# A sliding-window attention and mixture-of-depths kernel: the first batch by head groups, and the next batch's preparation spread over its blocks

## The chip, the cores and the metric

The kernel runs on one core of a Trainium2 chip. A core has five instruction streams: TensorE (PE in the profile, its weight loads PEld), VectorE (DVE), ScalarE (ACT), GpSimd (POOL) and SyncE (SP), which here only issues loads. The metric is the time of one execution on the device in microseconds (us); lower is better. The time of the kernel before is the median of three runs.

## The reference

Four batches, eight heads, 768 positions, head size 64. Attention sees a window of 128 positions and the first 4 positions ("sinks"). Then, per batch, the 128 rows with the highest gate score go through a two-layer MLP and are added back.

```python
scores = scale * np.matmul(q, k.transpose(0, 1, 3, 2))
keep = is_sink | in_window            # pos < 4, or 0 <= row - col < 128
scores = np.where(keep, scores, -1000000000.0)
a = softmax(scores)
x = np.matmul(a, v)                   # laid out (B, S, H * D) = (4, 768, 512)
...
scores = np.einsum('bsd,d->bs', x, w_gate)
out = x.copy()
for b in range(B):
    top_idx = np.argpartition(-scores[b], capacity)[:capacity]   # 128 rows
    xe = x[b, top_idx]
    ye = np.maximum(xe @ w1, 0.0) @ w2        # w1 512x1024, w2 1024x512
    g = 1.0 / (1.0 + np.exp(-scores[b, top_idx]))
    out[b, top_idx] = xe + g[:, None] * ye
```

## The kernel before

**Tiling.** A batch is worked in six blocks `j` of 128 positions, a step `(b, j)` of the main loop (lines 540 to 577) each, 24 in all. The eight heads are four pairs `hp`, and two groups `g` of four heads (pairs 0 and 1, pairs 2 and 3).

**Before a batch can start**, q and k of a head pair are loaded (`kf`, `qf`), cast to bf16 (`kb`, `qb`, lines 125 to 131: in batch 0 by ScalarE and VectorE, later by GpSimd, which uses an `affine_select` that selects everything as a copy), transposed by TensorE into PSUM (`trp`, line 252) and copied out as `KT` (VectorE, line 257) and `QT` (ScalarE, line 259). The first four columns of K^T go into `ksk` by two small VectorE copies for each pair (line 261).

**A step.** `scores` (lines 270 to 299) makes the score tile of the next block for both groups: products `sc` (line 282), masks added by a product with the identity (line 293), exp on ScalarE into `pt` (line 299). Then come the value products of this block: `pv_sinks` (line 316) with `psk`, the exp of the sink scores (`sink_scores`, lines 301 to 307, once per batch in block 0), and `vsk`, the sinks' values (`pack_sinks`, line 148); and `pv` (line 326), 64 products of 128 by 65 for both groups. VectorE divides by the sum (`rz` line 332, `x` line 335), GpSimd issues the write of `x` to the output (line 340), VectorE reduces `x` with the gate vector to a column of gate scores `scol` (line 347, `junk` is its unused product).

**Selection.** `compare` (lines 352 to 361) spreads a block's scores along the columns (`bc` on TensorE, `sbc` on ScalarE) and counts on VectorE who is larger (`cm`, `row`). `moe_steps` of the batch before runs in three steps: `cs` and the permutation `E` (line 377), then `se`, `idx` and the gather `xe`, then `xeT`. `mlp_steps` has two: `hps` (line 419), and `ye` (line 425) with the scattered addition. The steps are placed by hand: selection in blocks 1, 2 and 4; the MLPs at (2,4), (3,0), (3,1), (3,2), (3,4) and (3,5). The last batch's selection and MLP are `moe_last` (lines 435 to 509), the tail. `keep_warm` (line 77) issues matmuls whose result is not used.

**Order.** Each engine and SP's queue carry out their instructions in the order in which the program writes them. Start-up (lines 524 to 529) casts and transposes all four pairs and makes the scores of block 0. Pairs 0 and 1 of the next batch are cast and transposed in block 3, pairs 2 and 3 in block 4: the casts are written before the values of that block, the transposes after them (lines 552 to 564).

**Loads.** `load` lets only a few transfers be under way: a load waits until the third one before it (the fourth in batch 0) has landed. Batch 0 has q and k in pieces of two heads, all in front of v, which comes in six pieces of 128 positions with all heads; the two small loads of the sinks' values stand after v's second piece. Batches 2 and 3 load q and k in pieces of four heads. The buffers are 3 for q and k (four heads each) and 3 for weights; batch 3 has its weight loads around its q and k loads.

Of the kernel before, what the change touches and what calls it, by code (L numbers as in the profile page):

```python
# [9 lines left out]
FP32 = mybir.dt.float32  # L10
# [21 lines left out]
def kernel(  # L32
# [17 lines left out]
    ws = ctx.enter_context(tc.tile_pool(name="ws", bufs=3))  # L50
    qkp = ctx.enter_context(tc.tile_pool(name="qkp", bufs=3))
# [3 lines left out]
    pp = ctx.enter_context(tc.tile_pool(name="pp", bufs=3))  # L55
    xp = ctx.enter_context(tc.tile_pool(name="xp", bufs=4))
# [35 lines left out]
    def load_qk(b, parts):  # L92
        st = BatchState()
        st.b = b
        st.kq = {}
        st.qf, st.kf = [], []
        if b == 3:
            load_w(0)
            load_w(1)
        n = 4 // parts  # L100
        for g in range(2):
            for lst, nm in ((st.kf, "kf"), (st.qf, "qf")):
                lst.append(qkp.tile([128, 4, NB, D], FP32, name=nm, tag=nm))
            for i in range(parts):
                for src, lst in ((k, st.kf), (q, st.qf)):
                    h0 = 4 * g + n * i
                    load(
                        flight=4 if b == 0 else 3,
                        out=lst[g][:, n * i:n * i + n, :, :].rearrange("p h c d -> p h (c d)"),
                        in_=src[b, h0:h0 + n, :, :].rearrange("h (p c) d -> p h (c d)", c=NB))  # L110
        if b == 3:
            load_w(2)
            load_w(3)
        return st

    def casts(st, hp):
        kb = qbp.tile([128, NB, 2, D], BF16, name="kb", tag="kb")
        qb = qbp.tile([128, NB, 2, D], BF16, name="qb", tag="qb")
        h0 = 2 * (hp % 2)
        ks = st.kf[hp // 2][:, h0:h0 + 2, :, :]  # L120
        qs = st.qf[hp // 2][:, h0:h0 + 2, :, :]
        ko = kb[:, :, :, :].rearrange("p c h d -> p h c d")
        qo = qb[:, :, :, :].rearrange("p c h d -> p h c d")
        if st.b == 0:
            nc.scalar.copy(out=ko, in_=ks)  # L125
            nc.vector.tensor_copy(out=qo, in_=qs)
        else:
            for o, i in ((ko, ks), (qo, qs)):
                for e in range(2):
                    nc.gpsimd.affine_select(out=o[:, e, :, :], in_=i[:, e, :, :], compare_op=ALU.is_ge, fill=0.0,  # L130
                                            base=0, pattern=[[0, NB], [0, D]], channel_multiplier=0)
        st.kq[hp] = (kb, qb)

    def load_v(st):
        b = st.b
        st.v = vbuf[b % 2]
        st.vsk = vsk[b % 2]
        for c in range(NB):
            load(out=st.v[:, c, :, 0:D], in_=v[b, :, c * 128:(c + 1) * 128, :].rearrange("h p d -> p h d"),
                 flight=4 if b == 0 else 3)  # L140
            if c == 1:

                raw = vsr[b % 2]
                for R in range(2):
                    nc.sync.dma_start(out=raw[64 * R:64 * R + 4 * NSINK, :], in_=v[b, 4 * R:4 * R + 4, 0:NSINK, :])
# [6 lines left out]
    st0 = load_qk(0, 2)  # L152
# [21 lines left out]
    load_v(st0)  # L174


    trif = cp.tile([128, 3, 64], FP32, name="trif", tag="trif")
# [15 lines left out]
    iota_i = cp.tile([128, 128], I32, name="iota_i", tag="iota_i")  # L193
# [50 lines left out]
    def transposes(st, hp):  # L244
        if not hasattr(st, "QT"):
            st.QT = tp.tile([128, HP, S], BF16, name="QT", tag="QT")
            st.KT = tp.tile([128, HP, S], BF16, name="KT", tag="KT")
            st.ksk = ksk[st.b % 2]
# [11 lines left out]
        for e in range(2):  # L260
            nc.vector.tensor_copy(  # L261
                out=st.ksk[64 * e:64 * e + 64, hp, 8 * (hp % 2) + 4 * e:8 * (hp % 2) + 4 * e + 4],
                in_=st.KT[64 * e:64 * e + 64, hp, 0:NSINK])
# [6 lines left out]
    def scores(st, kc, g):  # L270
        nq = 256 if kc + 1 < NB else 128
        if g == 0:
            st.pt[kc] = pp.tile([128, H, 256], FP32, name="pt", tag="pt")
        pt = st.pt[kc]
# [22 lines left out]
        po = pt[:, 4 * g:4 * g + 4, :].rearrange("p (a e) n -> p e a n", e=2)  # L297
# [3 lines left out]
    def sink_scores(st):  # L301
        st.psk = sp.tile([128, 512], FP32, name="psk", tag="psk")
        sk = ps.tile([128, 512], FP32, name="sk", tag="ps")
        for hp in (0, 2, 1, 3):
            nc.tensor.matmul(out=sk[es[hp // 2], :], lhsT=st.ksk[:, hp, :], rhs=st.QT[:, hp, 256:S],
                             start=(hp % 2 == 0), stop=(hp % 2 == 1), skip_group_check=True)
        nc.scalar.activation(out=st.psk[:, :], in_=sk[:, :], func=ACT.Exp, scale=0.125)

    def pv_sinks(st, j):
        st.xg = [x_ps.tile([128, 4, VS], FP32, name="xg", tag="xg") for _ in range(2)]  # L310
        if j < 2:
            return
        for m in range(2):
            for g in range(2):
                q0 = (j - 2) * 128 + 64 * m
                nc.tensor.matmul(out=st.xg[g][es[m], :, :], lhsT=st.psk[es[g], q0:q0 + 64],  # L316
                                 rhs=st.vsk[es[g], :, :], start=True, stop=False, skip_group_check=True)

    def pv(st, j, g):
        xg = st.xg[g]  # L320
        terms = [(j, 0)] if j == 0 else [(j - 1, 128), (j, 0)]
        for hh in range(4):
            h = 4 * g + hh
            for kc, off in terms:
                for m in range(2):
                    nc.tensor.matmul(out=xg[es[m], hh, :],  # L326
                                     lhsT=st.pt[kc][:, h, off + 64 * m:off + 64 * m + 64],
# [5 lines left out]
        if g == 0:  # L333
            st.x = xp.tile([128, DM], FP32, name="x", tag="x")
        nc.vector.tensor_tensor(  # L335
            out=st.x[:, 256 * g:256 * g + 256].rearrange("p (h d) -> p h d", h=4),
            in0=xg[:, :, 0:D], in1=rz[:, :, :].to_broadcast((128, 4, D)), op=ALU.mult)

    def finish_block(st, j):
        nc.gpsimd.dma_start(out=out[st.b, j * 128:(j + 1) * 128, :], in_=st.x[:, :])  # L340
        if st.b == B - 1:
            if j == 0:
                st.xb = ws.tile([128, NB, DM], BF16, name="xb", tag="wf")
            nc.gpsimd.affine_select(out=st.xb[:, j, :], in_=st.x[:, :], compare_op=ALU.is_ge, fill=0.0,
                                    base=0, pattern=[[0, DM]], channel_multiplier=0)
        junk = sp.tile([128, DM], FP32, name="junk", tag="junk")
        nc.vector.tensor_tensor_reduce(  # L347
            out=junk[:, :], in0=st.x[:, :], in1=wgb[:, :], scale=1.0, scalar=0.0,
# [86 lines left out]
    def moe_last(st):  # L435
# [68 lines left out]
        yo = sp.tile([128, DM], FP32, name="yo", tag="junk")  # L504
# [7 lines left out]
    def start_state(st):  # L512
        st.pt = {}
        st.cm = {}
# [5 lines left out]
    units = [(b, j) for b in range(B) for j in range(NB)]  # L520
    with tc.manual_schedule(engines={ENG.PE, ENG.DVE, ENG.Activation, ENG.Pool, ENG.SP}):
        start_state(st0)
        keep_warm(10)
        for g in range(2):
            for hp in (2 * g, 2 * g + 1):
                casts(st0, hp)
                transposes(st0, hp)
                keep_warm(4)
            scores(st0, 0, g)
        gen = None  # L530

        def step():
            if gen is not None:
                next(gen, None)

        prep = {3: (0, 1), 4: (2, 3)}
        w_casts = {(2, 2): (0, 1), (2, 3): (2, 3), (2, 5): (4, 5), (3, 0): (6, 7)}
        mlp = {(2, 4): (0,), (3, 0): (0,), (3, 1): (1,), (3, 2): (1,), (3, 4): (2,), (3, 5): (2,)}
        mlps = {}
        for u, (b, j) in enumerate(units):  # L540
            st = states[b]
            if j == 0 and b + 1 < B:
                states[b + 1] = load_qk(b + 1, 2 if b == 0 else 1)
                load_v(states[b + 1])
            nxt = units[u + 1] if u + 1 < len(units) else None
            if nxt:
                if nxt[1] == 0:
                    start_state(states[nxt[0]])
                for g in range(2):
                    scores(states[nxt[0]], nxt[1], g)  # L550
            pv_sinks(st, j)
            hps = prep.get(j, ()) if b + 1 < B else ()
            for hp in hps:
                casts(states[b + 1], hp)
            for g in range(2):
                pv(st, j, g)
            if j == 1:
                pack_sinks(st)
            if j == 0:
                sink_scores(st)  # L560
            if j in (2, 4):
                step()
            for hp in hps:
                transposes(states[b + 1], hp)
            for i in w_casts.get((b, j), ()):
                cast_w(i)
            if u:
                pb, pj = units[u - 1]
                compare(states[pb], pj)
            if j == 1:  # L570
                step()
            for i in mlp.get((b, j), ()):
                next(mlps[i], None)
            finish_block(st, j)
            if j == 0 and b > 0:
                gen = moe_steps(states[b - 1])
                mlps[b - 1] = mlp_steps(states[b - 1])
        moe_last(states[B - 1])
# [35 lines left out]
```

## Time and profile before

| | us |
|---|---|
| median of 3 runs | 156.34 (154.6 to 157.71) |
| the profiled execution's own time | 159.9 |
| its span, first to last instruction | 158.2 |
| TensorE busy in it | 133.1 |
| VectorE busy | 108.0 |
| ScalarE busy | 82.5 |
| GpSimd busy | 60.5 |

The page gives busy time for each engine, the span in 40 slices (3.96 us each) with the busy share in tenths, the granted TensorE clock and the transfers, the chain of work that ended last, and groups of instructions by line with their mean time and with what ended the idle time in front of them. The trace behind it gives the same for any stretch, and a timeline. Of VectorE's 108.0 us, line 261 has 12.9 in 32 copies of 64x4 elements. The queue of loads moved 23.37 MB in 35440 packets, and 26096 of all 38413 packets are under 512 B. "Issue" as a releaser means that the profile shows nothing that the engine waited for.

### The profile page before, as it was taken

What the parts mean: (1) busy time and instruction counts of PE and PEld (TensorE: products, weight loads), DVE (VectorE), ACT (ScalarE), POOL (GpSimd) and SP (SyncE); (2) the same over time, 40 slices, a digit from 0 to 9 for tenths busy, and PEclk for the clock granted to TensorE, in tenths of its full rate; (3) what the DMA queues carried; (4) which work ended last, traced back from release to release, by engine and by line L of the source; (5) the groups of instructions that cost most, each with busy time, mean ns of one, the idle gap of its engine ahead of it and who ended that gap; (6) DMA issues with size and microseconds to landing.
All of it is one profiled execution on the core that took longest, in us unless ns stands there. A gap on an engine that the chain in (4) does not pass through costs nothing.

```text
span 158.2 us, 6573 instructions
## 1 busy us (share of the span) xinstructions
PE 133.1 (84%) x2857; PEld 100.8 (64%) x2857; DVE 108.0 (68%) x305; ACT 82.5 (52%) x168; POOL 60.5 (38%) x111
## 2 busy tenths in 40 slices
PE   6967999879599859883999975899899999999940
PEld 2533687768386657572878864698578777865810
DVE  3774356579987835999587879787959728667110
ACT  3456596553658505725375572769975464320310
POOL 7100011797111109941011199970446229207220
PEclk9997899999999987999599999599999999999998
DMA  4999989999899989999982139991108026405221
GB/s 162 322 331 200 220 271 343 286 297 229 167 385 389 311 187 213 394 386 374 339 312 77 70 51 321 278 216 45 68 2 193 15 37 109 161 4 67 70 66 66
DMA packets 38413, 31.78 MB, mean 201 GB/s; under 512 B 26096, under 2 KB 34672, under 8 KB 38384
## 3 DMA queue, kind: packets, MB, share of 16 engines
q1 hardware_dynamic: 35440, 23.37, 52.0%
q0 software_dynamic: 2944, 8.00, 17.1%
q8 instruction: 22, 0.36, 1.0%
q14 instruction: 7, 0.06, 0.1%
HBM read 24.41 MB, written 7.34 MB: 201 GB/s over the span
## 4 chain that ended last, share of the span: by engine, by line
PE 58%; DVE 14%; issue 12%; ACT 5%; POOL 4%; DMA 2%; POOLq 1%; ACTq 0%
PE xg L326 22%; PE w L77 8%; PE sc L282 5%; PE xg L316 5%; DVE KT L257 5%; DVE ksk L261 5%; PE trp L252 4%; PE hps L419 4%; PE ye L425 3%; PE sc L293 3%; ACT pt L299 2%; DVE x L335 2%; DMA xr<-out_dram,idx 2%; PE bc L354 2%; POOL qb L130 1%
## 5 line engine op out<-in xcount | busy, mean ns | idle before, releaser
L326 PEld LDWEIGHTS xg<-vbuf,pt 128*64 128x64 f32 x1408 | 45.3, 142 | 12.9 <-issue 11.7
L326 PE MATMUL xg<-vbuf,pt 128*64 128x65 f32 x1408 | 49.2, 228 | 3.8 <-issue 3.8
L299 ACT ACTIVATE pt<-sc 128x512 f32<-128x512 f32 (+1 forms) x96 | 46.6, 579 | 7.9 <-PE sc L293 7.8
L340 POOL DMA_DIRECT2D out_dram<-x x24 | 16.3, 679 | 59.0 <-DVE x L335 55.5
L332 DVE RECIPROCAL rz<-xg 128x4 f32<-128x4 f32 x48 | 8.6, 180 | 23.6 <-PE xg L326 23.1
L282 PE MATMUL sc<-QT,KT 64*64 64x192 bf16 (+3 forms) x384 | 19.2, 253 | 6.1 <-DVE KT L257 4.1
L358 DVE SCALAR_TENSOR_TENSOR cm<-sbc,scol,tie 128x128 bf16<-128x128 f32 (+5 forms) x24 | 19.3, 804 | 4.5 <-ACT sbc L355 4.5
L259 ACT COPY QT<-trp 128x768 bf16<-128x768 bf16 x16 | 12.4, 800 | 18.7 <-PE trp L252 18.7
L335 DVE TENSOR_TENSOR x<-xg,rz 128x256 f32<-128x256 f32 x48 | 20.4, 425 | 1.8
L347 DVE CUSTOM_DVE_ANT_0 junk<-x,wgb 128x512 f32<-128x512 f32 x24 | 20.2, 843 | 0.6 <-DMA wgb<-in_moe_w_gate_dram 0.6
L257 DVE COPY KT<-trp 128x768 bf16<-128x768 bf16 x16 | 15.3, 954 | 3.5 <-PE trp L252 3.2
L282 PEld LDWEIGHTS <-KT 64*64 64x64 bf16 x384 | 9.4, 108 | 12.2 <-issue 8.1
L293 PE MATMUL sc<-msk,ident_b 64*64 64x256 bf16 (+1 forms) x352 | 16.9, 252 | 0.0
L77 PE MATMUL w<-warm 128*128 128x512 bf16 x49 | 15.1, 454 | 1.3 <-DVE warm L72 1.3
L355 ACT COPY sbc<-bc 128x128 f32<-128x128 f32 x24 | 6.6, 275 | 14.1 <-PE bc L354 12.6
L261 DVE COPY ksk<-KT 64x4 bf16<-64x4 bf16 x32 | 12.9, 404 | 0.8
L130 POOL TENSOR_SCALAR_AFFINE_SELECT kb<-kf 128x384 bf16<-128x384 f32 x24 | 13.2, 576 | 0.1
L252 PE MATMUL trp<-ident_b,kb 128*128 128x128 bf16 x96 | 8.7, 231 | 5.1 <-ACT kb L125 2.7
L130 POOL TENSOR_SCALAR_AFFINE_SELECT qb<-qf 128x384 bf16<-128x384 f32 x24 | 12.9, 558 | 0.0
L316 PE MATMUL xg<-vsk,psk 64*64 64x260 f32 x128 | 12.1, 431 | 0.0
L252 PEld LDWEIGHTS <-kb 128*128 128x128 bf16 x96 | 6.3, 103 | 7.8 <-ACT kb L125 4.2
L293 PEld LDWEIGHTS <-ident_b 64*64 64x64 bf16 x352 | 10.3, 112 | 0.0
(99 smaller groups left out, 146.6 us busy)
## 6 DMA issues: line engine op xcount, KB each, us to landing
vbuf<-in_v_dram SPq DMA_DIRECT2D x24, 256.0 KB, 5.8
out_dram<-x POOLq DMA_DIRECT2D x24, 256.0 KB, 4.6
wf<-in_moe_w_dram SPq DMA_DIRECT2D x4, 1024.0 KB, 8.3
kf<-in_k_dram SPq DMA_DIRECT2D x8, 384.0 KB, 4.4
qf<-in_q_dram SPq DMA_DIRECT2D x8, 384.0 KB, 5.2
kf<-in_k_dram SPq DMA_DIRECT2D x4, 768.0 KB
qf<-in_q_dram SPq DMA_DIRECT2D x4, 768.0 KB
wgb<-in_moe_w_gate_dram SPq DMA_DIRECT2D x1, 256.0 KB
```

The source lines that it names most:

```text
L77: nc.tensor.matmul(out=w[:, :], lhsT=warm[:, 0:128], rhs=warm[:, :], start=True, stop=True)
L130: nc.gpsimd.affine_select(out=o[:, e, :, :], in_=i[:, e, :, :], compare_op=ALU.is_ge, fill=0.0, base=0, pattern=[[0, NB], [0, D]], channel ...
L252: nc.tensor.transpose(out=trp[:, c, :], in_=src[:, c, :, :].rearrange("p h d -> p (h d)"), identity=ident_b[:])
L257: nc.vector.tensor_copy(out=o, in_=i)
L261: nc.vector.tensor_copy(out=st.ksk[64 * e:64 * e + 64, hp, 8 * (hp % 2) + 4 * e:8 * (hp % 2) + 4 * e + 4], in_=st.KT[64 * e:64 * e + 64, h ...
L282: nc.tensor.matmul(out=sc[e][es[kh], hh, q0:q1], lhsT=st.KT[es[e], hp, k0:k0 + 64], rhs=st.QT[es[e], hp, kc * 128 + q0:kc * 128 + q1], sta ...
L293: nc.tensor.matmul(out=sc[e][es[kh], :, 64 * s0:64 * s1].rearrange("p h (s n) -> p h s n", n=64), lhsT=ident_b[es[e], es[e]], rhs=m[es[e], ...
L299: nc.scalar.activation(out=po[:, e, :, 0:nq], in_=sc[e][:, :, 0:nq], func=ACT.Exp, scale=0.125)
L316: nc.tensor.matmul(out=st.xg[g][es[m], :, :], lhsT=st.psk[es[g], q0:q0 + 64], rhs=st.vsk[es[g], :, :], start=True, stop=False, skip_group_ ...
L326: nc.tensor.matmul(out=xg[es[m], hh, :], lhsT=st.pt[kc][:, h, off + 64 * m:off + 64 * m + 64], rhs=st.v[:, kc, h, :], start=(j < 2 and hh ...
L335: nc.vector.tensor_tensor(out=st.x[:, 256 * g:256 * g + 256].rearrange("p (h d) -> p h d", h=4), in0=xg[:, :, 0:D], in1=rz[:, :, :].to_bro ...
L347: nc.vector.tensor_tensor_reduce(out=junk[:, :], in0=st.x[:, :], in1=wgb[:, :], scale=1.0, scalar=0.0, op0=ALU.mult, op1=ALU.add, accum_ou ...
```

## The change

Batch 0 runs twice through its six blocks, first for heads 0 to 3 and then for heads 4 to 7. A new function `unit(b, j, gs)` is a step for the groups `gs`; for batch 0 it is called with one group, for the others with both. Start-up casts and transposes pairs 0 and 1 alone; pairs 2 and 3 of batch 0 are cast in blocks 3 and 4 of the first pass and transposed in front of the values of its block 5. The loads follow: q and k of pairs 0 and 1, the sinks' values, v of heads 0 to 3 in half pieces, q and k of pairs 2 and 3, v of heads 4 to 7. The loads of batch 1 are written between the two passes.

In the later batches the casts of a next pair stand at blocks 2, 3, 4 and 5, one pair each. Pair 0 is transposed in block 3 and pair 1 in block 4, in front of that block's values; pairs 2 and 3 in block 5, behind them. The next batch's block 0 has its scores in two parts: group 0 in front of the values of block 5, group 1 at the very end of that step. The `ksk` copies go from VectorE to GpSimd. All q and k loads are of two heads, with 4 buffers; the weights have 4 buffers and their loads stand behind batch 3's q and k, ahead of its v. Selection steps are in blocks 1, 2 and 3, that of block 2 in front of its values. The MLP halves are at (3,0), (3,1), (3,2) twice, (3,3) and (3,4), and the weight casts at (2,5) and (3,0), four each. `pt` is a tile for one group (6 buffers), `x` has 8 buffers, `xg` and its sink products are made for one group at a time, `junk` is bf16, and `trif`, `iota_i` and `yo` use the buffers of `x`.

```diff
+    def load_batch(st):
+        for hp in range(HP):
+            load_qk(st, hp)
+        if st.b == B - 1:
+            for i in range(4):
+                load_w(i)
+        for c in range(NB):
+            load_v(st, c, slice(0, H))
+            if c == 0:
+                load_sinks(st)
...
+    load_sinks(st0)
+    for g in range(2):
+        if g:
+            for hp in (2, 3):
+                load_qk(st0, hp)
+        for c in range(NB):
+            load_v(st0, c, slice(4 * g, 4 * g + 4))
...
         for e in range(2):
-            nc.vector.tensor_copy(
+            nc.gpsimd.affine_select(
                 out=st.ksk[64 * e:64 * e + 64, hp, 8 * (hp % 2) + 4 * e:8 * (hp % 2) + 4 * e + 4],
-                in_=st.KT[64 * e:64 * e + 64, hp, 0:NSINK])
+                in_=st.KT[64 * e:64 * e + 64, hp, 0:NSINK], compare_op=ALU.is_ge, fill=0.0,
+                base=0, pattern=[[0, NSINK]], channel_multiplier=0)
...
+    cast_at = {2: 0, 3: 1, 4: 2, 5: 3}
+
+    layers_mid = {(3, 0): 0, (3, 2): 1}
+    layers_late = {(3, 1): 0, (3, 2): 1, (3, 3): 2, (3, 4): 2}
+    w_casts = {(2, 5): range(0, 4), (3, 0): range(4, 8)}
+
+    def unit(b, j, gs):
+        st = states[b]
+        last = 1 in gs
+        nst, nj = (st, j + 1) if j + 1 < NB else (states.get(b + 1), 0)
+        ahead = states.get(b + 1) if last else None
+        if ahead and j in cast_at:
+            casts(ahead, cast_at[j])
+        if j + 1 < NB:
+            for g in gs:
+                scores(st, j + 1, g)
+        elif ahead:
+            scores(ahead, 0, 0)
+        if ahead and j in (3, 4):
+            transposes(ahead, j - 3)
+        if b and j == 2:
+            next(select[b - 1])
+        for g in gs:
+            pv(st, j, g)
+        if j == 0:
+            sink_scores(st, gs)
+        if j == 1 and gs[0] == 0:
+            pack_sinks(st)
+        if b and j == 1:
+            next(select[b - 1])
+        if b and j == 3:
+            next(select[b - 1], None)
+        if (b, j) in layers_mid:
+            next(mlp[layers_mid[b, j]], None)
+        if ahead and j == 5:
+            transposes(ahead, 2)
+            transposes(ahead, 3)
+        if not last:
+            return
+        if j or b:
+            compare(*((st, j - 1) if j else (states[b - 1], NB - 1)))
+        if (b, j) in layers_late:
+            next(mlp[layers_late[b, j]], None)
+        for i in w_casts.get((b, j), ()):
+            cast_w(i)
+        finish_block(st, j)
+        if ahead and j == 5:
+            scores(ahead, 0, 1)
...
+        for hp in range(2):
+            casts(st0, hp)
+            transposes(st0, hp)
+            keep_warm(3)
+        scores(st0, 0, 0)
         for g in range(2):
...
+            if g:
+                states[1] = new_state(1)
+                start_state(states[1])
+                load_batch(states[1])
+            for j in range(NB):
+                if g == 0 and j >= 3:
+                    if j < 5:
+                        casts(st0, j - 1)
+                    else:
+                        transposes(st0, 2)
+                        transposes(st0, 3)
+                unit(0, j, (g,))
+            if g == 0:
+                scores(st0, 0, 1)
```

## The prediction

> **What bounds the kernel now.** I read first the slices of the page (its second part), then a table of busy time for six stretches that I cut by hand, then the list of waits, and last the timeline of VectorE and GpSimd where batch 1 hands over to batch 2.
>
> ```profile
> PE   6967999879599859883999975899899999999940
> PEclk9997899999999987999599999599999999999998
> DMA  4999989999899989999982139991108026405221
> ```
>
> TensorE is the busiest engine (84%), but it has dents in every batch, and behind a dent the granted clock falls too. The transfers are full until slice 22 (87 us) and then have room. The stretches below are: start-up; batch 0 to the start of batch 1's second score block; the same step for batches 1 and 2; batch 3 to its last value product; tail.
>
> ```profile
> 0.00:19.50 19.50, 15.27 (x138) 8.20 (x138) 10.34 (x38) 9.66 (x14) 3.41 (x21) 0.91 0.95 248
> 19.50:45.50 26.00, 22.53 (x602) 18.54 (x596) 18.88 (x54) 15.71 (x34) 11.21 (x21) 1.00 0.95 273
> 45.50:79.80 34.30, 27.69 (x662) 22.25 (x662) 25.78 (x70) 16.99 (x37) 12.20 (x23) 0.90 1.02 329
> 79.80:110.80 31.00, 27.52 (x690) 22.59 (x690) 26.21 (x70) 20.67 (x42) 16.45 (x26) 0.94 0.61 167
> 110.80:139.30 28.50, 27.20 (x658) 21.47 (x658) 20.33 (x57) 16.37 (x37) 12.30 (x15) 1.00 0.34 81
> 139.30:158.20 18.90, 12.88 (x124) 7.74 (x124) 6.41 (x19) 3.07 (x7) 4.89 (x5) 0.97 0.23 57
> ```
>
> Columns: length, busy TensorE (matmuls, weight loads), VectorE, ScalarE, GpSimd, clock, transfer share, GB/s. Until 19.5 us TensorE does next to nothing that counts (the first value product starts there, because all four head pairs must be loaded, cast and transposed first). In batch 1 it idles 6.6 us and works at clock 0.90; in batch 3 it idles 1.3 us.
>
> ```profile
> DVE rz L332 <- PE xg L326: 23.1, 28, 2.7
> PE sc L282 <- DVE KT L257: 4.1, 4, 1.6
> PE xg L326 <- issue: 3.8, 4, 2.2
> PE trp L252 <- POOL kb L130: 1.6, 2, 1.2
> ```
>
> VectorE mostly waits for TensorE (23.1 us); TensorE waits for the transposes' copies and GpSimd's casts around each hand-over, and 3.8 us for nothing that the profile shows.
>
> ```profile
> 63.62 1.01 POOL L130 TENSOR_SCALAR_AFFINE_SELECT qb<-qf 128x384 bf16<-128x384 f32 x2
> ...
> 68.10 1.02 POOL L130 TENSOR_SCALAR_AFFINE_SELECT qb<-qf 128x384 bf16<-128x384 f32 x2
> ...
> 63.88 0.95 DVE L257 COPY KT<-trp 128x768 bf16<-128x768 bf16 x1
> 64.86 4.28 DVE L261 COPY ksk<-KT 64x4 bf16<-64x4 bf16 x2
> ```
>
> Two 64x4 copies that otherwise take 0.17 us each last 4.28 us, exactly until GpSimd's row of casts ends at 69.1. The K^T copy, whose source is PSUM, ran at its usual 0.95 us beside the same casts.
>
> **What the Trainium skill says.** "SBUF — State Buffer", Who interferes with whom: a VectorE copy in a two-port mode, or a VectorE operation with two SBUF inputs, excludes GpSimd for a whole instruction, and the loser waits. The 4.28 us agree. "Runtime: NRT & Kernel Launch", Instruction fetch mechanics: instructions come in blocks of 256. The four unexplained waits (at 31.24, 50.21, 54.81 and 83.91 us) lie, by a table of stretches cut at these times, 765, 255 and 1020 matmuls and weight loads apart, close to 3, 1 and 4 blocks, so I take them for late fetches under full transfers. "TensorE: Matmul & The Clock Gate", What's actually happening: an idle TensorE loses clock. The dents of 7, 5 and 5 follow idle stretches here. "DMA: Bandwidth & Descriptors", Why small descriptors are slow: transfers in pieces of 256 B, as those of v are (64 floats), lose throughput to a fixed cost of each. The slice where v loads begin has 200 GB/s against 322 and 331 before it.
>
> **The change, by stretch.**
>
> *Batch 0 (45.5 us now).* The first q and k loads are unchanged, so the first score block is at 10.4 as now. Then heads 0-3 run alone. ScalarE's chain: two exps 1.09, cast 0.83, psk 0.63, Q^T copy 0.80. From 11.04: exp 0 to 12.1, exp 1 13.2, psk 13.9, exp 2 15.0, exp 3 16.1, cast 16.9, exp 4 18.0, cast 18.9, exp 5 (half) 19.5. TensorE per half block: scores 0.45, sinks 0.22, values 1.01 (half of 2.02), so it follows: value product 0 at 12.2, product 4 to 19.3, transposes of pairs 2 and 3 to 20.7, product 5 to 21.9. Heads 4-7: scores of two blocks from 22.0 to 22.9, exp done and first product at 23.7, then 0.76 (block 0 with sink scores), 1.71 (block 1), 1.93 (block 2), 2.61 and 2.44 (blocks 3 and 4 with one pair's transposes, 0.68 each), 4.63 (block 5: scores 0.45, values 1.23, two pairs 1.35, bc 0.25, wait for pair 3's K^T 0.9, scores 0.45): 14.1, end 37.8. One late fetch of 1.05 as now: **38.9, a gain of 6.6**.
>
> The half pieces of v are not in this trace: 128 KB lands within half of to all of the 5.1 us that 256 KB takes. With both small sink loads in front (1.1 us of issue each) v pieces are issued from 5.0 on; pair 3's loads, behind them, then land between 15.5 and about 21, and their cast is due at 18. So 0 to 3 us; I take 0 and keep 3 for the range. Bytes: by 39 us q, k, v of batch 0 (4.7 MB), gate 0.26, q and k of batch 1 (3.1), a first v piece 0.26 and five outputs 1.3 are due: 9.7 MB. The page's first ten slices moved 10.5. That is 3 us of room.
>
> *Batches 1 and 2.* Full-clock TensorE work is 27.69 x 0.90 = 24.9 and 27.52 x 0.94 = 25.9; the latter loses the first MLP's first half (1.95): 23.9. Casts come one pair a block (4 x 0.55) and, for pairs 0 to 2, one block before their transposes, which hides them; pair 3's are cast and transposed in block 5 and hidden by values (2.5). If GpSimd were late there the full 2.05 would show. The small copies on GpSimd: 32 x 0.19 (the nearest row, a 64x4 select) = 6 us, 1.5 a batch; on its in-order queue they hold the next output and cast back, but it waits 55.5 us for x, so nothing to 0.6 a batch; I take nothing. VectorE loses 5.24 and 3.79 us there. New waits: the selection product moves in front of block 2's values. It needs E: after block 1's last product VectorE does x (0.7), vsk 0.42, two rows 0.33, E 0.96, two rid 0.35 = 2.7; TensorE has cs 0.35, bc 0.25, scores 0.9 = 1.5 to do. It waits 1.2 (bounds 0 and 2.7), and behind it stand the values of block 2. And pair 3's K^T copy: 0.9 (0 to 1.7), with the next batch's scores behind it. Kept: fetches 2.5 and 0.3, and half of the clock loss (1.5 and 0.8). Sum: 24.9+1.2+0.9+2.5+1.5 = **31.0 (now 34.3)**; 23.9+1.2+0.9+0.3+0.8 = **27.1 (now 31.0)**.
>
> *Batch 3 (28.5).* It takes one hps more (1.95) and the last ye out of the tail (1.75): 27.2+3.7 = 30.9; idle 1.3 kept; the selection wait 1.2; two weight casts on ScalarE (2 x 1.05) now precede exps of its first block: 1.4 (0 to 2.1). **34.8.** Fourth weight buffer: SP's wait of 16.1 us for a cast goes, and v of batch 3 comes behind 4 MB of weights: from about 60 us, 8.7 MB at 350 GB/s is 25 us, and with 1.6 MB of outputs 30, before 97 when batch 3 begins. Nothing.
>
> *Tail (18.9).* Without ye the 7 warm matmuls end at 141.3 rather than 142.9 and junk's 141.4 decides: 1.4; rid (0.81 beside GpSimd's cast, else 0.17) 0.6. **16.9.** Buffers, junk in bf16 and one dummy matmul fewer per pair: nothing, VectorE and the loads cover them.
>
> Sum 38.9+31.0+27.1+34.8+16.9 = **148.7** against the span of 158.2 (that execution's time was 159.9, 2.3% over the median). 9.5 less from the median of 156.34 is **146.8**.
>
> **Rivals.** *Arrivals*: loads, not order, set batch 0 and its gain of 6.6 goes; 155.3 of span, 153.4. For it: transfers at 9 throughout; against: the 0.8 MB of room. *Old waits return*: batches 1 and 2 keep 34.3 and 31.0, since fetches and clock made them; 154.0. For it: 2.2 of the 6.6 idle us in batch 1 are one fetch. *Slower*: GpSimd's burst now follows each x, just where VectorE runs cm and junk, both with two SBUF inputs; junk already averages 843 ns against 0.69 undisturbed. If the 2.05 us of each of 12 bursts reach TensorE, 24.6 are added: 171.4. It decides from 1.06 us a burst: 2% over the median is 159.5, in span 161.4, and (161.4-148.7)/12 is that. Against it: 8.5 us of VectorE idle in batch 1, three xg buffers, and ksk gone. *More*: no late fetches (3.8) and full clock (2.3): 140.7.
>
> **Chances.** Forecast 0.60 (own range 143 to 151), arrivals 0.10, old waits 0.13, slower 0.07, more 0.10. The range 141 to 155 holds all but the slower case and the ends. A measurement of this kernel tells about 2% from no change (153.2 and 159.5). Half of *arrivals* and a third of *old waits* fall below 153.2 (0.05 and 0.04): faster 0.60+0.10+0.09 = 0.79, within 0.14, slower 0.07.
>
> **What would show it.** First value product near 12 us instead of 19.5; batch 1's scores of block 1 near 39; no 64x4 copy on VectorE; TensorE's wait for kb gone and one for E in front of se, near 1.2 us, in three batches; tail near 17. Wrong if first products wait for v, or if VectorE's junk grows past 1.5 us and TensorE waits for x or K^T.

## The result and the profile after

The changed kernel takes **166.9 us** (median of four runs, 165.8 to 168.0) against 156.24 for the kernel before (now four runs); the ratio is 1.072, with a 95% interval of 1.058 to 1.086. I had forecast 146.8, and faster. Executions of one kernel spread by several per cent, so medians below are of all runs while ratios compare only the fast runs of each kernel (within 1.5% of its fastest), and where the two differ the ratio counts. The profiled execution took 167.77 us, its span is 166.1; that of the kernel before took 159.9, 3.7 over its median. So the table shows a loss of 7.9 where the medians show 10.7, and a miss of 17.4 where they show 20.1. By the stretches of the prediction (us of span):

| stretch | before | forecast | after | after minus forecast |
|---|---|---|---|---|
| batch 0 | 45.5 | 38.9 | 45.5 | +6.6 |
| batch 1 | 34.3 | 31.0 | 32.5 | +1.5 |
| batch 2 | 31.0 | 27.1 | 33.9 | +6.8 |
| batch 3 | 28.5 | 34.8 | 35.9 | +1.1 |
| tail | 18.9 | 16.9 | 18.3 | +1.4 |
| span | 158.2 | 148.7 | 166.1 | +17.4 |

The slices of the changed kernel, which answer to those shown of before:

```profile
PE   6779898989788799997969999986999989979950
PEclk9969999999999969999996599999999999999996
DMA  5969788999999999989899979300304326043021
```

TensorE is now busier (87% against 84%), as meant. But it is busy with more: 144.4 us instead of 133.1, with ten instructions fewer. So the loss is not in waits: TensorE idles 21.7 us, 25.1 before. The groups of instructions of the changed kernel say where (busy us and mean ns, then the idle time in front):

```profile
L325 PEld LDWEIGHTS xg<-vbuf,pt 128*64 128x64 f32 x1408 | 47.1, 143 | 16.2 <-issue 13.4
L325 PE MATMUL xg<-vbuf,pt 128*64 128x65 f32 x1408 | 53.3, 231 | 0.9 <-ACT pt L301 0.9
L318 PE MATMUL xg<-vsk,psk 64*64 64x260 f32 x128 | 21.7, 415 | 0.7 <-ACT pt L301 0.7
L346 DVE CUSTOM_DVE_ANT_0 junk<-x,wgb 128x512 bf16<-128x512 f32 x24 | 19.7, 823 | 0.0
```

and two of the kernel before:

```profile
L326 PE MATMUL xg<-vbuf,pt 128*64 128x65 f32 x1408 | 49.2, 228 | 3.8 <-issue 3.8
L316 PE MATMUL xg<-vsk,psk 64*64 64x260 f32 x128 | 12.1, 431 | 0.0
```

The 128 sink records take 21.7 us, and the same 128 took 12.1 before; the value products went from 49.2 to 53.3. One sink record lasts no longer than before (415 ns, 431 before). What fell is how many are under way at a time: 128 x 0.431 / 12.1 gives 4.6 before, 128 x 0.415 / 21.7 gives 2.4 now. `junk` has not grown (823 ns, before 843), so my "slower" rival is not what happened. The wait of 3.8 us in front of value products for nothing that the profile shows is gone too. The chain of waits of the changed kernel (start, duration, what) shows block 2 of batch 1 from its wait on, and after the gap block 3:

```profile
54.35 0.45 DVE rid L381
54.83 0.45 DVE rid L382
55.32 0.41 PE se L388 x11
55.73 0.59 PE xg L318 x4
56.32 1.08 PE xg L325 x32
57.40 0.81 PE xg L318 x4
58.21 1.93 PE xg L325 x32
...
62.51 0.59 PE xg L318 x4
63.09 1.08 PE xg L325 x32
64.17 0.58 PE xg L318 x4
64.76 1.08 PE xg L325 x32
```

and the chain of the kernel before shows a block of batch 0:

```profile
42.85 0.44 PE xg L316 x8
43.29 2.02 PE xg L326 x64
```

Before, sinks and values of a block took 0.44 + 2.02 = 2.46 us; now 0.59 + 1.08 + 0.58 + 1.08 = 3.33. That is 0.87 us a block, on the path that sets the end, and there are 16 blocks with sinks: 13.9 us at most, since a few first runs stand right behind scores and take 0.44. My forecast had 2 x (0.22 + 1.01), no more than before. At 57.40 the second thing shows: behind the wait for `rid` in front of `se`, the same work takes 0.81 and 1.93 instead of 0.58 and 1.08, and the clock has a 6 in this slice (the fifteenth, 58 to 62 us).

### The profile page after: what moved, and what is told of

Its sections match the earlier page's. It is cut to its first block, busy times and chain, and to the rows that moved or that the text cites. A ratio compares the mean times of both kernels' runs of the same rounds, so it can differ in the third digit from the quotient of the medians.

```text
span 166.1 us, 6606 instructions
## 1 busy us (share of the span) xinstructions
PE 144.4 (87%) x2847; PEld 104.2 (63%) x2847; DVE 93.3 (56%) x273; ACT 83.4 (50%) x169; POOL 70.1 (42%) x143
## 4 chain that ended last, share of the span: by engine, by line
PE 66%; ACT 10%; DMA 6%; DVE 6%; issue 5%; POOL 3%; SPq 1%; POOLq 1%; DVEq 0%; ACTq 0%
PE xg L325 27%; PE xg L318 11%; PE trp L255 5%; ACT pt L301 5%; PE sc L284 5%; DMA qf<-in_q_dram 4%; PE hps L418 3%; PE w L77 3%; PE ye L424 3%; PE sc L295 3%; ACT QT L262 2%; DMA xr<-out_dram,idx 2%; PE bc L353 1%; POOL qb L139 1%; POOL kb L139 1%
## 5 line engine op out<-in xcount | busy, mean ns | idle before, releaser
L325 PEld LDWEIGHTS xg<-vbuf,pt 128*64 128x64 f32 x1408 | 47.1, 143 | 16.2 <-issue 13.4
L325 PE MATMUL xg<-vbuf,pt 128*64 128x65 f32 x1408 | 53.3, 231 | 0.9 <-ACT pt L301 0.9
L339 POOL DMA_DIRECT2D out_dram<-x x24 | 15.7, 656 | 33.9 <-DVE x L334 20.9
L284 PE MATMUL sc<-QT,KT 64*64 64x192 bf16 (+3 forms) x384 | 20.0, 259 | 4.8 <-ACT pt L301 2.3
L357 DVE SCALAR_TENSOR_TENSOR cm<-sbc,scol,tie 128x128 bf16<-128x128 f32 (+5 forms) x24 | 17.5, 729 | 9.4 <-ACT sbc L354 9.1
L318 PE MATMUL xg<-vsk,psk 64*64 64x260 f32 x128 | 21.7, 415 | 0.7 <-ACT pt L301 0.7
L354 ACT COPY sbc<-bc 128x128 f32<-128x128 f32 x24 | 6.6, 276 | 27.2 <-PE bc L353 27.1
L346 DVE CUSTOM_DVE_ANT_0 junk<-x,wgb 128x512 bf16<-128x512 f32 x24 | 19.7, 823 | 0.0
L262 ACT COPY QT<-trp 128x768 bf16<-128x768 bf16 x16 | 12.6, 804 | 13.4 <-PE trp L255 13.3
L264 POOL TENSOR_SCALAR_AFFINE_SELECT ksk<-KT 64x4 bf16<-64x4 bf16 x32 | 7.4, 232 | 25.6 <-DVE KT L260 24.7
L284 PEld LDWEIGHTS <-KT 64*64 64x64 bf16 x384 | 9.3, 110 | 12.1 <-issue 8.0
L139 POOL TENSOR_SCALAR_AFFINE_SELECT kb<-kf 128x384 bf16<-128x384 f32 x24 | 16.1, 690 | 0.5
L77 PE MATMUL w<-warm 128*128 128x512 bf16 x39 | 12.3, 463 | 1.3 <-DVE warm L72 1.3
L428 POOL DMA_INDIRECT out_dram<-gye,idx x3 | 4.9, 1644 | 16.1 <-ACT gye L427 12.9
L295 PEld LDWEIGHTS <-ident_b 64*64 64x64 bf16 x352 | 10.7, 114 | 0.0
```

The source lines that it names most:

```text
L77: nc.tensor.matmul(out=w[:, :], lhsT=warm[:, 0:128], rhs=warm[:, :], start=True, stop=True)
L262: nc.scalar.copy(out=o, in_=i)
L284: nc.tensor.matmul(out=sc[e][es[kh], hh, q0:q1], lhsT=st.KT[es[e], hp, k0:k0 + 64], rhs=st.QT[es[e], hp, kc * 128 + q0:kc * 128 + q1], sta ...
L295: nc.tensor.matmul(out=sc[e][es[kh], :, 64 * s0:64 * s1].rearrange("p h (s n) -> p h s n", n=64), lhsT=ident_b[es[e], es[e]], rhs=m[es[e], ...
L318: nc.tensor.matmul(out=xg[es[m], :, :], lhsT=st.psk[es[g], q0:q0 + 64], rhs=st.vsk[es[g], :, :], start=True, stop=False, skip_group_check= ...
L325: nc.tensor.matmul(out=xg[es[m], hh, :], lhsT=st.pt[kc, g][:, hh, off + 64 * m:off + 64 * m + 64], rhs=st.v[:, kc, h, :], start=(j < 2 and ...
```

## Experiments

### What a run of sink products costs

*Both groups' sinks together* (a1), and the same in another order (a2): the values stay by group, batch 0 stays as changed.

```diff
+    def pv_sinks(st, j, gs):
+        st.xg = {g: x_ps.tile([128, 4, VS], FP32, name="xg", tag="xg") for g in gs}
+        if j < 2:
+            return
+        for m, g in [(m, g) for m in range(2) for g in gs]:    # a2: for g in gs for m in range(2)
...
+        pv_sinks(st, j, gs)
         for g in gs:
             pv(st, j, g)
```

> The changed kernel, with the sink products of both groups of batches 1 to 3 put together in front of the block's values again, alternating between the groups (first half of group 0, first half of group 1, then the second halves); batch 0 stays as changed. Row theory: two sink products in a row that take different halves of TensorE's rows run side by side, two that share a half run one after the other; the changed order costs 2 x (0.585 + 1.08) = 3.33 us a block against 0.44 + 2.02 = 2.46. 12 blocks x 0.87 = 10.4 us come back: 156.5. Rival (the loss lies in the new wait in front of se, the clock behind it and the casts): 165 or more, and a block's values still start 0.58 us after its sinks.

> As the run with paired sinks, but each group's two halves follow one another (group 0, group 0, group 1, group 1), all four in front of the values. It tells the order from the number of changes between 64-row and 128-row weights, which is one a block here and two in the changed kernel. Row theory: the four still run mostly one after the other, about 0.9 us a block instead of 0.44; only the second change of weights (about 0.15 a block) and the values' 0.14 are saved: 163 to 164. Rival (the changes cost it all): as the paired run, 156 to 157.

Measured: a1 157.21 (20 runs; ratio to before 1.007, 1.002 to 1.012), a2 157.26 (20 runs; 1.014, 1.009 to 1.019). So this one step makes up 9.7 us of the 10.7 that the change lost. The row theory fails in a2, for which it expected 163 to 164: the order inside a run makes no difference clear of noise (the intervals overlap, and eight records take 0.60 and 0.44 in a2's chain too); that it is one run decides. The chain of a1:

```profile
63.78 0.60 PE xg L320 x8
64.38 2.02 PE xg L330 x64
66.39 0.25 PE bc L358
66.65 0.34 PE sc L284 x6
66.98 0.17 PE sc L295 x8
67.15 0.44 PE xg L320 x8
```

Each of these products leaves two records, so a run of four products has eight. They take 0.60 behind other products and 0.44 right behind scores, no more than four records took. By stretches a1 is 44.0, 28.4, 30.7, 33.1 and 18.3: batches 1 to 3 are 10.1 us shorter than in the changed kernel, for 12 blocks times 0.87 = 10.4.

*One product of 128 columns of weights for each group instead of two of 64* (a3: `lhsT=st.psk[es[g], q0:q0 + 128]`, `out=xg[:, :, :]`), and *the kernel before with each group's sinks in front of its own values* (b1):

> The changed kernel, with the two sink products of a group made one of 128 columns (they have the same values as the moving operand); the order stays by group. If a product of 128 columns costs what one of 64 costs, a group's sinks take about 0.29 us instead of 0.585 in all 16 blocks: 9 us less, 157 to 158. If it costs twice as much, since fp32 products are split in passes, nothing changes: 166 to 167.

> The kernel before with nothing changed but the sinks: each group's two sink products stand directly in front of that group's values, as in the changed kernel. Row theory: 16 blocks x 0.87 us = 13.9 slower, 170. Rival (sinks cost nothing, the loss is elsewhere in the change): within 2% of the kernel before, 155 to 159.

Measured: a3 169.68 (ratio 1.084, 1.073 to 1.095); half as many sink instructions, and a run lasts 0.63. b1 163.7 (four runs, 160.5 to 164.5) against 156.8: the split alone costs the kernel before 6.9 us by the medians and 6.6 by the lowest runs (before 153.8); no interval can be given. Its blocks grow by the same 0.87 (0.58 and 1.08 in its chain), but half of the 13.9 disappears in slack, of which the waits show a part: TensorE's wait for the K^T copy falls from 4.1 to 1.5 us and its unexplained wait from 3.8 to 2.6, while that for ScalarE's casts of k grows from 2.7 to 4.0.

What is the 0.58 made of? Half the columns (c1, `xg[es[m], 0:2, :]`, `vsk[es[g], 0:2, :]`), and 128 rows instead of 64 (c2: `psk` twice, each with zeros in the other group's rows, `lhsT=st.psk[g][:, q0:q0 + 64]`, `rhs=st.vsk[:, :, :]`; besides, one more exp for each of batches 1 to 3, and six `x` buffers instead of eight):

> The changed kernel, with each sink product cut to the first two heads of its group: 130 columns instead of 260 (the sinks' values of heads 2 and 3 of each group are left out). It asks what the 0.58 us of a run of sink products is. Streaming theory: a run lasts as long as its 260 columns take to pass twice, the four quadrants of the array pass theirs side by side, and the change fills only two of the four at a time; then half the columns take some 0.19 us off each of the 32 runs, 6 us in all: 161. Change theory: the run costs a fixed time for going from one kind of product to the other; then the runs stay at 0.45 to 0.60 and the time at 166 to 168.

> The changed kernel, with sink products of 128 rows: each group has its own copy of the exps, with zeros in the other group's 64 rows, so sinks and values have the same number of rows. (Six x buffers instead of eight, since the copies need room; one exp of 64 rows more per batch on ScalarE.) Change theory: the 0.39 us gap of the weight loads between sinks and values goes, and with it some 0.2 to 0.4 us for each of 32 runs: 155 to 160. Streaming theory: the 260 columns still pass twice for each of two products, now without a neighbour in the other rows: the run stays near 0.55 and the time at 165 to 168.

Measured: c1 159.7 (1.032, 1.022 to 1.042), c2 163.25 (1.057, 1.045 to 1.068). The chains of c1 and then of c2, one block each:

```profile
65.59 0.37 PE xg L318 x4
65.96 1.08 PE xg L325 x32
67.05 0.37 PE xg L318 x4
```

```profile
68.60 0.59 PE xg L320 x4
69.19 0.93 PE xg L327 x32
70.12 0.44 PE xg L320 x4
```

Both theories hold a part. With 130 columns a run takes 0.37 instead of 0.58: 0.21 for 130 columns, so by my estimate 0.42 of the 0.58 is columns passing. The 32 runs then save 6.7 us, and the time falls by 7.2. With 128 rows a run behind values takes 0.44 instead of 0.58 (one behind transposes or scores takes 0.59), and the values behind it 0.93 instead of 1.08; their weight loads hardly wait for nothing shown any more (13.4 us in the changed kernel, 1.9 in c2). So going from 64 rows to 128, or back, costs some 0.15 us each time. A block of c2 takes 0.59 + 0.93 + 0.44 + 0.93 = 2.89, and of the 0.87 us about a half (0.44) is change of rows and the other half (0.43) that two runs stream their columns one after the other, which in one run pass side by side. This split is read from the blocks of the chain; the whole time of c2 falls by 3.7 us (2.4 by the ratios), not by 16 x 0.44 = 7.0. A part of the rest shows: a run right behind scores takes 0.59 in c2 where the changed kernel has 0.44, and TensorE waits in c2 1.4 us for a cast of k, 1.2 for `psk` and 0.7 in front of value products for nothing shown. The Trainium skill names both, the change and the running side by side: "TensorEngine Tiling (Array Packing)", Key Properties of its Tiling Modes: changing the mode drains TensorE, and tiles work in parallel. It gives no price; these runs do.

### The wait for E and the clock behind it

*se behind the values of block 2* in batches 1 and 2 (d1, from a1), and besides *the sinks directly behind the scores, ahead of the transposes* (g1, from d1):

```diff
-        if b and j == 2:
+        if b == 3 and j == 2:
             next(select[b - 1])
...
-        if b and j == 3:
+        if (b in (1, 2) and j == 2) or (b, j) in ((1, 4), (2, 4), (3, 3)):
             next(select[b - 1], None)
```

> The changed kernel with the sinks of both groups together (157.2 in its run) and, in batches 1 and 2, the selection product se behind the values of block 2 instead of in front of them, the transposed rows in block 4. If the wait for E (1.35 us, twice) and the clock that falls behind it are what batch 2 lost against the forecast, it gains 2.7 for the waits and 2 to 4 for the clock: 151 to 153. If the gather of the selected rows, which stood in the chain of the run before, sets the pace, the later se makes it later still and the time stays at 156 to 158.

> The version of 154.5 (sinks of both groups together, se behind the values of block 2 in batches 1 and 2), with the sink products directly behind the scores, in front of the transposes, so that products of 64 rows follow each other. If a run of sinks costs 0.15 us more for coming behind products of 128 rows, six runs gain 0.9 and the time is 153.6. If only the streaming of the columns counts, it stays at 154.5.

Measured: d1 154.51 (4 runs; ratio 0.997, 0.984 to 1.010), g1 157.08 (22 runs; 1.002, 0.999 to 1.006). Neither gives what I expected. Four runs are too few to say whether d1 gains anything over a1. g1, of which there are more, gains little, but it also differs from d1 in the order of its sinks, so it does not decide for d1. In g1's profile the waits for E are gone, and TensorE waits 2.4 us for nothing shown in front of value products, which in a1 it did not. g1 is no proof against the 0.15 for a change of rows either: six times 0.15 is less than these runs differ by.

### The small key copies

*Back on VectorE* (f1, from a1) and *on ScalarE* (f2, from a1):

```diff
-            nc.gpsimd.affine_select(
-                out=st.ksk[...], in_=st.KT[...], compare_op=ALU.is_ge, fill=0.0, base=0, ...)
+            nc.vector.tensor_copy(out=st.ksk[...], in_=st.KT[...])     # f2: nc.scalar.copy
```

> The changed kernel with the sinks of both groups together (157.2 in its run), and the small key copies back on VectorE. If they still run beside GpSimd's casts there, as in the kernel before (12.9 us for 32), they last 9 to 13 us, K^T copies and x behind them come later, and the time rises by 1 to 3: 158 to 160. If the casts, now one pair a block, leave VectorE alone, the copies last 5.5 us (0.17 each) and the time stays at 157; if GpSimd's own 7.1 us for them were what made the casts late (TensorE waits 1.0 for qb), it falls to 156.

> The changed kernel with the sinks of both groups together (157.2 in its run), and the small key copies on ScalarE, neither on GpSimd nor on VectorE. If VectorE had to be rid of them (171.1 with them there), it is 157 to 160: 32 copies of some 0.2 us lie on ScalarE. If what counts is that GpSimd's copies wait for K^T and so hold the next casts back until VectorE has done its x, cm and junk, the casts come early here too, junk again lasts up to 2.8 us, TensorE waits for K^T as with the copies on VectorE (9.4 us), and it is 166 to 171.

Measured: f1 171.12 (1.095, 1.087 to 1.103), f2 170.09 (1.095, 1.086 to 1.103), both against 157.2. I had costed this step at nothing for GpSimd, and 5.24 and 3.79 us less on VectorE; without it 13 to 14 us are lost. It cannot be only the time of the copies on VectorE: in f2 it has none. The timeline of f2 (start, duration, engine, what, and in brackets the wait in front) at the end of batch 2, where the row of casts is longest:

```profile
104.99 0.55 POOL L343 DMA_DIRECT2D out_dram<-x  x1 [1.41 <-PE sc L294]
105.28 4.80 DVE L350 CUSTOM_DVE_ANT_0 junk<-x,wgb 128x512 bf16<-128x512 f32 x1
105.55 1.04 POOL L139 TENSOR_SCALAR_AFFINE_SELECT kb<-kf 128x384 bf16<-128x384 f32 x2
106.53 1.02 POOL L139 TENSOR_SCALAR_AFFINE_SELECT qb<-qf 128x384 bf16<-128x384 f32 x2
107.50 2.02 POOL L242 TENSOR_SCALAR_AFFINE_SELECT w_sb<-wf 128x1024 bf16<-128x1024 f32 x2
...
112.11 0.30 PE L283 MATMUL sc<-QT,KT 64*64 64x256 bf16 x4 [1.58 <-DVE KT L260]
```

and of a1 at the same place of batch 1, with the copies on GpSimd:

```profile
67.38 0.55 POOL L344 DMA_DIRECT2D out_dram<-x  x1 [1.25 <-PE sc L295]
67.67 0.69 DVE L351 CUSTOM_DVE_ANT_0 junk<-x,wgb 128x512 bf16<-128x512 f32 x1
67.98 1.27 POOL L139 TENSOR_SCALAR_AFFINE_SELECT kb<-kf 128x384 bf16<-128x384 f32 x2
69.21 1.02 POOL L139 TENSOR_SCALAR_AFFINE_SELECT qb<-qf 128x384 bf16<-128x384 f32 x2
```

GpSimd issues the output of x, and 0.29 us later `junk` begins; the casts follow. In a1 they begin 0.60 us behind the issue, `junk` takes 0.69 and the first cast pair is the one that is held (1.27 instead of 1.04). In f2 they begin 0.55 to 0.56 behind it and are not held, and `junk` lasts until the whole row of casts has ended: 4.80 us. In both `junk` has begun before the casts. At the four places of a1 and of the changed kernel where `junk` begins 0.28 or 0.29 behind the issue, the casts begin 0.60 or 0.61 behind it and `junk` takes 0.69; at the five such places of f1 and f2 they begin 0.55 or 0.56 behind it, and `junk` takes 2.81 three times, 4.79 and 4.80. (That a VectorE operation with two SBUF inputs, as `junk` is, contends with GpSimd for a pair of ports under an exclusive lock is what the Trainium skill states in "SBUF — State Buffer", Who interferes with whom; these durations agree.) The K^T copy stands behind `junk`, the next batch's scores behind that: TensorE waits 9.4 us for K^T in f1, 1.6 at the place shown of f2 (3.2 in all of it). That is the mechanism of my "slower" rival, and with the copies on GpSimd it does not appear. But these waits are not the whole 13 to 14 us. TensorE is busy 138.7 us in f1 and 136.0 in f2 against 131.0 in a1, at a granted clock of 0.92 and 0.94 against 0.98. And f2 has a loss of its own kind:

```profile
ACT ksk L264 <- DVE KT L260: 12.9, 7, 3.3
```

ScalarE's copies wait for K^T and hold what it does next; TensorE waits 2.8 us for Q^T there, 1.0 in a1. How the loss of f2 divides between the two is open. My own wording for f2, that GpSimd's copies wait for K^T and hold the casts back, is only half right: what the trace shows is 0.05 us. Why the casts begin 0.05 us later with the copies in that queue no run here shows, and that these 0.05 us decide is read from nine places, not tested.

### Batch 0 by groups

*v waits for the second pair's keys* (d2, from a1: the first piece of v waits for the second load before it instead of the fourth); *batch 0 whole* (h1, from a1: start-up, loads and steps of batch 0 as in the kernel before):

> The changed kernel with the sinks of both groups together (157.2 in its run); the first piece of v waits until the second pair's keys have landed, so that it no longer travels beside the keys and queries of the first two pairs. If v overtaking them is why the first scores came 1.6 us late, they come near 10.5 and the time falls by 1 to 1.6: 155.5 to 156.2. If v is then what comes late, the first value products wait and the time stays at 157 or above.

> The changed kernel with the sinks of both groups together (157.2 in its run), and batch 0 with both groups in each block, all of q and k loaded first and v in whole pieces, as in the kernel before. If the order by groups is worth what the stages say (batch 0's step ends at 43.95 in that run and at 45.5 in the kernel before), the time rises by 1.5 to 158.7. If the earlier first product only brings the loads of batch 1 into the way and the eight separate sink runs eat the rest, it stays at 157 or falls to 156.

Measured: d2 158.51 (1.015, 0.993 to 1.037), h1 156.67 (21 runs; 0.991, 0.986 to 0.995). What d2 was to cure is not there in a1. The first scores of d2 come at 10.4, but those of a1, where v may travel beside q and k as in the changed kernel, come at 10.6, and those of the eight other versions with these loads at 10.1 to 10.9. Only the profiled execution of the changed kernel was late (12.0). Its chain, then that of a1:

```profile
9.96 0.82 PE trp L255 x6
10.78 1.28 PE w L77 x3
12.06 0.56 PE sc L284 x6
```

```profile
9.51 0.51 PE trp L255 x6
10.02 0.65 PE w L77 x3
10.67 0.21 PE sc L284 x2
```

The same work takes longer, under the 6 of the clock's third slice; 0.45 us more come from a later arrival of q. So v is not shown to be the cause. In d2 batch 0 ends at 43.8 instead of 44.0. In h1 the first value product comes at 18.7 instead of 12.1, and batch 0 ends at 44.2. So 6.6 us of earlier start give nothing; by the ratios of h1 and a1 (0.991 and 1.007) the whole batch 0 is even 2.6 us better. Over all of batch 0 TensorE is busy 37.1 us in a1 and 36.3 in h1, and h1 has idle time of another cause in it, one line of its waits:

```profile
DVE junk L348 <- DMA wgb<-in_moe_w_gate_dram: 4.0, 1, 4.0
```

The gate weights stood behind all of v in SP's queue. Loaded behind v's first piece (k1), then with five dummy matmuls in front of `se` in batches 1 and 2 (k2, `keep_warm(5)`), or with `se` behind the values there as in d1 (k3):

> The version with batch 0 whole (156.7), the gate weights loaded behind the first piece of v instead of behind all six. There VectorE's gate product waited 4.0 us for them in batch 0 and TensorE 2.2 us behind it. If that wait is all that stands there, batch 0 ends 2 us earlier, near 42, and the time is 154.5: the order by groups then costs 2 us against a whole batch. If v or the loads of batch 1 come later instead, batch 0 still ends at 44 and the time stays at 156 to 157.

> The same with the early gate weights, and five dummy matmuls in front of se in block 2 of batches 1 and 2, where TensorE otherwise waits 1.4 us for E. The wait stays, only the clock can gain: if the clock falls because of this wait (64 value products took 3.64 us instead of 2.02 behind it), it gains 1.6 once or twice over the version without them: 151.5 to 153. If the clock falls for another reason, no gain: 154.5.

> The same with the early gate weights, and se behind the values of block 2 in batches 1 and 2 (no dummy matmuls). If the wait for E costs its own 1.7 us, twice, and the clock behind it besides, it gains 3 to 5 over the version with se in front: 150 to 151.5. If late fetches and the gather of rows take the place of that wait, as the 157.1 of the version by groups with the late se suggests, it gains 0 to 1: 153.5 to 154.5.

Measured side by side: k1 155.37 (22 runs; 0.990, 0.987 to 0.994), k2 155.81 (22; 0.988, 0.984 to 0.993), k3 **153.76** (14; 0.984, 0.979 to 0.988). k1 gains 1.3 over h1 by the medians, but its ratio is that of h1 (0.990 and 0.991), so a gain from the early gate weights is not shown; in its profile batch 0 ends at 43.0. What is clear of noise is that a whole batch 0 is better than one by groups, with the gate weights early or late. k2 filled the wait, and in its timeline the 64 value products behind `se` took 2.09 both times, where k1 had 3.13 and a1 3.64 in batch 2; still its time is k1's. In that profile TensorE waits 1.4 us for nothing shown in front of value products; whether that is what took the gain back is open. k3 gains 1.0 by the ratios and 1.6 by the medians over k1, less than the 3 to 5 expected, and the intervals touch. Its span by stretch (length, busy TensorE, loads, VectorE, ScalarE, GpSimd, clock, transfer share, GB/s):

```profile
0.00:42.40 42.40, 35.28 (x731) 25.00 (x735) 25.10 (x78) 24.71 (x45) 17.88 (x58) 1.00 0.96 263
42.40:69.61 27.21, 24.96 (x669) 20.15 (x661) 22.07 (x62) 16.60 (x37) 15.88 (x32) 1.00 0.92 259
69.61:99.89 30.28, 25.30 (x668) 20.23 (x661) 21.99 (x62) 16.84 (x38) 16.37 (x33) 1.00 0.96 310
99.89:132.98 33.09, 30.77 (x708) 23.79 (x698) 18.89 (x55) 21.20 (x43) 15.74 (x18) 1.00 0.38 86
132.98:151.30 18.32, 11.17 (x116) 6.94 (x116) 6.86 (x19) 2.39 (x6) 5.16 (x7) 0.91 0.25 72
```

The clock is full up to the tail, and TensorE's work in batches 1 and 2 is 25.0 and 25.3 us; the forecast took 24.9 and 23.9. TensorE waits in this profile 1.3 us in front of value products and 1.1 in front of transposes for nothing shown. k3 is the best version found: 1.6% faster than the kernel before, 7.9% faster than the changed one by the medians.

## Why the prediction was wrong

The step that failed is the term "sinks 0.22, values 1.01 (half of 2.02)" for a half block in batch 0, together with what I did not write down at all for batches 1 to 3: in the diff the sink products moved from one run for both groups into `pv`, and I costed that at nothing. I halved a run, where halving leaves its time as it is: the columns of four products pass side by side, and there is a change of rows at each end. Measured, the half block costs 0.58 + 1.08, and a block 0.87 us more than the 2.46 before: at most 16 times 0.87 = 13.9 us of the 17.4 that the span missed by. For the 12 blocks of batches 1 to 3 a1 shows it (10.1 us); for the 3.5 us of batch 0 it rests on the durations. Each other point:

- *Batch 0* (forecast 38.9, measured 45.5). Eight half blocks with sinks cost up to 0.43 more each, 3.5 us; the first scores came at 12.0 instead of 10.4, which is bad luck of this execution, since the other versions with these loads have them at 10.1 to 10.9 as forecast; TensorE waits 1.0 for the q casts. I had read the 7 us of an earlier start as a gain less added work; but with it batch 0 ends at 44.0 (a1) and 43.8 (d2), without it at 44.2 (h1) and 43.0 (k1). How much of the gain the added runs took and how much idle time took back is open.
- *Batch 1* (31.0, measured 32.5) was close by luck: 4 x 0.87 = 3.5 more, and the late fetches (2.5) that I kept did not come. Without the split it takes 28.4.
- *Batch 2* (27.1, measured 33.9): 3.5 for the split; the wait for E 1.35 and 0.3, near my 1.2; and behind it the clock, of which I had kept 0.8: its block 2 takes 0.85 + 1.93 + 1.06 + 1.93 = 5.77 instead of 3.33 us.
- *Batch 3* (34.8, measured 35.9): 3.5 for the split, less the wait for E, which did not come since `ye` stands in front of it. The weight casts held scores 1.6 us, forecast 1.4. That the miss is only 1.1 is therefore luck: these terms alone give 2.5, and what took the rest back I cannot say.
- *Tail* (16.9, measured 18.3): of my gain of 1.4 from taking `ye` out 0.4 came: TensorE's `cs` now waits 1.2 us for `cm`, which `ye` used to hide, and the 7 warm matmuls and the last `bc` stand behind it; `junk` besides took 1.32 beside a GpSimd cast, 0.69 before. `rid` took 0.17 instead of 0.81, as forecast.
- *Small key copies on GpSimd*: their own cost was right (232 ns, forecast 190; 7.4 us in all, nobody waits), and VectorE's stalls went. The size was off: without this step the rest of the change would cost 13 to 14 us more (f1 and f2 against a1).
- *Rivals.* Arrivals: the chain has q of the second pair, 7.00 us, only at the start. Old waits: the late fetches did not come back here. Slower: right in mechanism, absent in the changed kernel, present in f1 and f2.

The change is thus a sum of a loss that I had not seen (the split sinks), a gain that I overrated (batch 0) and a step that I underrated (the copies). This step is no gain of 14 us over the kernel before, which takes 156 with the copies on VectorE: it averts a loss that the rest of the change would bring.

## What to carry to other kernels

When a loop is split, look at each short run of products inside it: work that used only part of the array side by side with its neighbour does not get cheaper by halves, and each change between 64 and 128 rows costs again. Price a run by what its columns take to pass, not by its number of instructions. And where two engines exclude each other, ask who comes first: here casts that began 0.05 us earlier went with 2.8 and 4.8 us in place of 0.7.

## What the hardware showed that I had not expected

- A run of fp32 sink products of 64 rows by 260 columns took 0.58 to 0.60 us with four records and with eight, 0.63 with two of double width, 0.37 with 130 columns, 0.44 right behind other products of 64 rows. Going from 64 rows to 128, or back, added some 0.15.
- Behind a wait of 1.36 us the next 64 value products took 3.64 us in batch 2 of a1 and 2.09 in batch 1, with the same wait in front. With the wait filled they took 2.09 in both, in the one profiled execution of k2.
- A VectorE reduction of 0.69 us lasted 4.80 us beside four GpSimd casts in a row and two more of double length, and took 0.69 in a1, where the casts began 0.05 us later.
